# An attention and mixer kernel on one core: another order on SyncE's queue, another scratch for one PSUM copy, one eviction a place earlier, another last piece

## The chip, the cores and the metric

The kernel runs on one core of one Trainium2 chip. The metric is the device time of one execution in microseconds (us), lower is better; a kernel's figure is the median of its runs. Engines are named as the profile names them: PE is TensorE's matmul, PEld its weight loads, DVE is VectorE, ACT is ScalarE, POOL is GpSimd, SP is SyncE. "SPq", "ACTq" and "POOLq" are the queues from which an engine issues DMAs.

## The reference

Two layers in a row, over 8 batches (B), 12 heads (H), 448 tokens (S) and 64 channels a head (D):

```python
def _attn_ref(q, k, v):
    S = q.shape[2]
    scale = 1.0 / np.sqrt(q.shape[-1])
    scores = scale * np.matmul(q, k.transpose(0, 1, 3, 2))
    attn = np.maximum(scores, 0.0) ** 2 / S
    return np.matmul(attn, v)

def _moe_ref(x, w_tok1, w_tok2, w_ch1, w_ch2):      # x: 8 x 448 x 768
    xt = x.transpose(0, 2, 1)
    h = np.maximum(xt @ w_tok1, 0.0) @ w_tok2       # 448 -> 256 -> 448, along the tokens
    u = x + h.transpose(0, 2, 1)
    h2 = np.maximum(u @ w_ch1, 0.0) @ w_ch2         # 768 -> 1536 -> 768, along the channels
    return u + h2
```

The attention has no softmax: a score is cut at zero and squared. Its heads side by side are the 768 channels of x. Inputs and output are float32; the kernel computes in bfloat16 with float32 sums in PSUM.

## The kernel before

**The work.** The heads are taken in 24 groups of four (s = 0 to 23), three groups to a batch. The batches b = 0 to 7 go in pairs p = 0 to 3; a pair has 7 tiles of 128 token rows in the channel layer, 28 over the kernel. The order of all work is written out by hand: `ORDER`, a string of 2024 words, is read from left to right, and each word issues one step on the engine that it names (`:A` on ACT, `:D` on DVE, digits are PSUM banks of a matmul). Each engine runs its steps in that order, with semaphore waits for what each step needs.

**The words.** For a group s:

- `ldk`, `ldq`, `ldv` load k, q and v from POOL (line 371); a name behind a load's colon is a gate: the load is issued once that DMA has landed.
- `ik`, `iq` put k and q in the right layout (ACT or DVE, line 351), `xk`, `xq` transpose them by a DMA on SP (line 497). Groups 0 to 9 are transposed on PE instead.
- `S` are the scores (PE, line 515), `r` their eviction with the cut at zero (line 343 or 345), `q` the squares (355 or 357), `V` the product with v (542), `xe` its eviction (552 or 554).
- `xd` transposes x by a DMA on SP (line 566, tile `x_sb`), from group 6 on; `t1` (PE, line 588) needs it. `rt`, `t2` (597) and `u` (DVE, line 601, tile `uT`) finish the token layer.
- `ub` copies u back into token rows by a DMA transpose on SP (line 610, tile `u_sb`, in the last pair a part of `arena`).

The channel layer's first product is plain for batches 0 and 1 (`C1`, line 623) and a Strassen-like scheme with seven products for the rest (`fast1`): `tu` are sums of u (DVE, line 688), `M1` the products (PE, line 780), `s1` copies of a product from PSUM into a scratch as float32 (ACT, line 793), `d1` the additions that use such a copy and the next product (DVE, line 796). The sums `tu3.0` are made in place in `uT`, so they wait for the `ub` copies of the same u. The second product (`fast2`) takes the tiles of a pair two by two: `h` are sums (688), `M2` products (847), `d2` evictions into the output tile (860 and 862). One tile in seven has no partner (`channel2`): `C2` (PE, line 713) and `c2e` (DVE, line 722). `st` are the stores (line 668), two for a tile of 128 rows, both on SP; in the last pair some are split by columns, and then one half goes from ACT's queue. The tile that ends the list, number 25, is computed in three pieces of columns: `C2.3.4.0` (384 wide), `.1` (256) and `.2` (128).

**SP's queue.** SP issues 152 DMAs in the order of the words: 94 transposes (`xk`, `xq`, `xd`, `ub`) and 58 copies, nearly all of them stores. It is one queue: a DMA whose data isn't there yet holds up those behind it, and each also waits until the DMA eight places ahead of it has landed, since eight semaphores go round.

**Scratch.** The tile `sums` holds, in its last columns, a scratch for a copy of `fast1` (`snaps[0]`, 2 x 448 float32) which shares its place with one of the `tu` sums. In the last pair the array `r2`, the scratches and the sums lie in `arena`, where k, q and their like were. There `fp32(4)` is a view of rows 4 and 5 of `r2`, and the built program's waits go by the stretch of memory that a view spans.

Of the kernel before, what the change touches and what calls it, by code (L numbers as in the profile page):

```python
# [115 lines left out]
V7.2 V7.3 V7.4 r8.6.1:A st1.64 V7.5 c1e1.2:D r8.6.0:A V7.6 S8.4:21 T9.0:56 xe7.1:A r8.4.1:A xe7.0:A S8.1:37  # L116
cp9.0:D C1.1.5:4 r8.1.1:A xd7 r8.1.0:D cp9.1:A C1.1.10:1 r8.4.0:A c1e1.5:D ub1.3 st1.0 q8.2:D S8.5:50 r8.5.1:A
w1.1.1:D S9.0:37 S9.4:64 r8.5.0:A ldv9.0:xd6 ub1.1 xk11 C1.1.9:2 c1e1.9:A r9.4.0:D ldv10.1:st2.64 C1.1.6:0
q8.6:D r9.0.1:A r9.0.0:D w1.1.0:D c1e1.10:D r9.4.1:A C1.1.3:5 xq11 q9.0:D q8.4:D t1.6.0:6 q9.4:A q8.5:A
t1.7.0:3 ldq13.0:st1.0 rt6.0:A iq12:D ub1.2 c1e1.6:A ldk12.1:st1.64 ldq13.1:xd7 c1e1.3:D S9.2:27 rt7.0:A  # L120
S9.3:41 q8.1:D q8.3:D V8.0:56 r9.2.0:D r9.3.0:A V8.1 V8.2 r9.2.1:D S9.1:03 r9.3.1:A V8.3 S9.5:24 r9.1.0:A
r9.1.1:D V8.4 ldk14.0:xk11 S10.1:71 V8.5 r9.5.1:A V8.6 S9.6:03 r9.5.0:D xe8.0:D ldk12.0 ldk15.1 r9.6.0:A
q9.2:A t2.7.0:4 q9.5:D ldk13.0:st1.0 r9.6.1:A C1.1.11:2 q9.1:D ldq15.1 q9.3:A C1.1.7:5 t2.6.0:0 ldk13.1:xq11
q9.6:A xe8.1:D w1.1.2:D r10.1.0:D t2.6.1:3 c1e1.11:A u7.0:D C1.1.8:6 r10.1.1:A u6.0:D q10.1:A c1e1.7:D ub2.0
S10.0:74 V9.0:20 V9.1 V9.2 V9.3 r10.0.0:D c1e1.8:A S10.3:15 u6.1:D V9.4 S10.4:76 xq12 r10.3.1:A ik12:D V9.5
V9.6 h0.3.0:D r10.4.1:A M2.0.3.2:3 xe9.0:D r10.4.0:A st0.0 ub2.1 r10.3.0:A xe9.1:A r10.0.1:D S10.5:56
d2.0.3.11a:D S11.0:72 S11.3:14 q10.3:D r10.5.1:A h0.3.1:D M2.0.3.1:0 r10.5.0:A r11.3.1:D xd8 r11.3.0:A
# [24 lines left out]
q13.4:A M2.1.4.2:5 q13.6:A u10.0:D rt12.0:D xk16 V13.0:32 V13.1 ldq18.0:st3.0 ldk19.0 h1.4.0:D S14.4:17
# [93 lines left out]
def kernel(ctx: ExitStack, tc: tile.TileContext, q: bass.AP, k: bass.AP, v: bass.AP, moe_w_tok1: bass.AP, moe_w_tok2: bass.AP, moe_w_ch1: bass.AP, moe_w_ch2: bass.AP, out: bass.AP):  # L246
    nc = tc.nc
    B, H, S, D = q.shape
# [681 lines left out]
    reads1, reads2 = ({}, {})  # L930
# [73 lines left out]
```

## Time and profile before

| | |
|---|---|
| median of 3 runs | 344.83 us (343.36 to 346.12) |
| the profiled execution, its time | 344.91 us |
| its span, from the first to the last instruction | 342.9 us |
| mean granted TensorE clock | 0.999 |
| PE busy | 333.5 us, 97% of the span |
| DVE, ACT, POOL busy | 295.0, 250.2, 92.0 us (86%, 73%, 27%) |
| PE idle that the waits name | 4.5 us |
| DMA queue of SP and ACT (q1) | 26.92 MB, 44.8% of 16 engines' span |
| DMA queue of POOL (q0) | 21.47 MB, 45.8% |
| out_dram<-out_sb from SP | 42 stores of 192 KB, 3.5 us to landing |
| transposes from SP, u_sb, arena, x_sb | 4.7, 4.7, 5.3 us to landing |

PE is the engine to look at: it is idle for under 10 us of the span. A row of the timeline has the start, the duration, the engine, the line, what is written and read, and in brackets how long the engine had been idle and what ended that. The ends of matmuls are modelled, so a matmul's row ends later than the next one can start; the distance between two starts says more. "DMA share" over 1 means that more packets were under way than there are engines.

### The profile page before, as it was taken

The numbers are of one execution on the slowest core, as the hardware profiler recorded it, in microseconds if no ns is written. First come the engines' busy times: TensorE is split into PE (matmuls) and PEld (weight loads), VectorE is DVE, ScalarE is ACT, GpSimd is POOL, SyncE is SP. The second block draws the span as 40 slices with busy tenths as digits, with TensorE's granted clock in tenths as the row PEclk, the third lists the DMA queues.
The fourth block names the chain that finished last, engine by engine and source line by source line (L and its number), as shares of the span: only waits on it lengthen the run. The fifth ranks groups of instructions, "written<-read, shape, count | busy, mean of one in ns | idle before, by whom it ended". The sixth has DMA issues, their size and how long they took to land.

```text
span 342.9 us, 9412 instructions
## 1 busy us (share of the span) xinstructions
PE 333.5 (97%) x3797; PEld 222.1 (65%) x3797; DVE 295.0 (86%) x571; ACT 250.2 (73%) x462; POOL 92.0 (27%) x157
## 2 busy tenths in 40 slices
PE   8899999999999999999999999999999999999995
PEld 3456655655565658855578556876578777887763
DVE  3999998899899999989898999889986986838783
ACT  4999999858899799879799898979785832221000
POOL 8976422725160343122340712010020000000000
PEclk9999999999999999999999999999999999999999
DMA  8999999999998999999999997897686113432255
GB/s 143 187 176 190 205 210 193 136 153 146 207 184 150 198 132 160 160 208 151 189 171 196 160 179 134 159 151 128 125 135 102 25 31 79 90 80 62 70 149 153
DMA packets 98940, 50.20 MB, mean 146 GB/s; under 512 B 71568, under 2 KB 95952, under 8 KB 98896
## 3 DMA queue, kind: packets, MB, share of 16 engines
q0 software_dynamic: 25136, 21.47, 45.8%
q1 hardware_dynamic: 72736, 26.92, 44.8%
q10 hardware_dynamic: 1024, 1.21, 1.2%
q8 instruction: 29, 0.48, 0.6%
q14 instruction: 15, 0.12, 0.1%
HBM read 43.38 MB, written 11.01 MB: 159 GB/s over the span
## 4 chain that ended last, share of the span: by engine, by line
PE 85%; DMA 5%; POOL 4%; DVE 3%; issue 1%; ACT 1%; SPq 0%; DVEq 0%; ACTq 0%; POOLq 0%
PE m_ps L847 22%; PE m_ps L780 20%; PE sc_ps L515 10%; PE acc_ps L542 8%; PE m_ps L623 8%; PE t_ps L588 6%; PE h_ps L597 5%; PE m_ps L713 4%; POOL arena L371 3%; DMA u_sb<-uT 2%; DMA x_sb<-xT 2%; PE kqT_ps L472 1%; DMA arena<-in_q_dram 1%; PE x_ps L579 1%; DVE arena L796 1%
## 5 line engine op out<-in xcount | busy, mean ns | idle before, releaser
L343 ACT ACTIVATE arena<-sc_ps 128x448 bf16<-128x448 f32 x232 | 117.1, 592 | 17.4 <-PE sc_ps L515 16.8
L355 ACT ACTIVATE arena<-arena 128x896 bf16<-128x896 bf16 x76 | 72.3, 968 | 0.6 <-DVE arena L345 0.3
L345 DVE TENSOR_SCALAR arena<-sc_ps 128x448 bf16<-128x448 f32 x104 | 62.1, 616 | 3.7 <-PE sc_ps L515 3.1
L515 PE MATMUL sc_ps<-arena 64*64 64x448 bf16 x672 | 54.8, 357 | 1.9 <-ACT arena L349 0.8
L357 DVE TENSOR_TENSOR arena<-arena 128x896 bf16<-128x896 bf16 x92 | 55.1, 616 | 1.1 <-ACT arena L343 0.5
L371 POOL DMA_DIRECT2D arena<-in_q_dram x46 | 28.2, 615 | 75.3 <-DMA arena<-arena 28.8
L371 POOL DMA_DIRECT2D arena<-in_v_dram x48 | 29.3, 618 | 66.2 <-DMA arena<-arena 17.5
L780 PEld LDWEIGHTS <-wc 128*128 128x128 bf16 x432 | 40.9, 98 | 5.1 <-issue 2.3
L542 PE MATMUL acc_ps<-arena 64*64 64x448 bf16 x672 | 42.7, 350 | 0.2
L515 PEld LDWEIGHTS <-arena 64*64 64x64 bf16 x672 | 21.7, 105 | 23.9 <-issue 15.4
L371 POOL DMA_DIRECT2D arena<-in_k_dram x48 | 29.7, 623 | 19.4 <-DMA out_dram<-out_sb 9.7
L780 PEld LDWEIGHTS <-ws 128*128 128x128 bf16 x324 | 30.8, 98 | 4.0 <-issue 1.8
L847 PE MATMUL m_ps<-wc,r 128*128 128x384 bf16 x162 | 30.3, 327 | 0.0
L601 DVE TENSOR_TENSOR uT<-h_ps,xT 128x448 bf16<-128x448 f32 x48 | 29.1, 616 | 1.2 <-PE h_ps L597 0.9
L847 PEld LDWEIGHTS <-r 128*128 128x128 bf16 x216 | 20.4, 98 | 14.8 <-issue 2.6
L623 PE MATMUL m_ps<-uT,wc 128*128 128x448 bf16 x144 | 29.9, 353 | 0.0
L542 PEld LDWEIGHTS <-arena 64*64 64x64 bf16 x672 | 20.9, 106 | 11.3 <-issue 3.1
L793 ACT ACTIVATE arena<-m_ps 128x448 f32<-128x448 f32 x18 | 9.3, 542 | 23.7 <-PE m_ps L780 8.3
L588 PE MATMUL t_ps<-x_sb,wt 128*128 128x256 bf16 (+1 forms) x216 | 25.0, 261 | 0.9 <-DMA x_sb<-xT 0.9
L780 PE MATMUL m_ps<-uT,wc 128*128 128x224 bf16 x216 | 25.4, 259 | 0.0
L597 PE MATMUL h_ps<-wt,r_sb 128*128 128x448 bf16 x96 | 25.1, 353 | 0.0
L847 PEld LDWEIGHTS <-sums 128*128 128x128 bf16 x180 | 17.1, 98 | 12.1 <-issue 1.0
(86 smaller groups left out, 510.1 us busy)
## 6 DMA issues: line engine op xcount, KB each, us to landing
out_dram<-out_sb SPq DMA_DIRECT2D x42, 192.0 KB, 3.5
arena<-in_k_dram POOLq DMA_DIRECT2D x48, 112.0 KB, 5.1
arena<-in_v_dram POOLq DMA_DIRECT2D x48, 112.0 KB, 5.2
arena<-in_q_dram POOLq DMA_DIRECT2D x46, 112.0 KB, 4.8
wc<-in_moe_w_ch_dram POOLq DMA_DIRECT2D x6, 768.0 KB, 11.5
out_dram<-arena SPq DMA_DIRECT2D x4, 192.0 KB, 2.7
out_dram<-out_sb SPq DMA_DIRECT2D x8, 96.0 KB, 2.1
out_dram<-out_sb ACTq DMA_DIRECT2D x8, 96.0 KB, 2.4
```

The lines of the kernel that those rows point to most:

```text
L343: nc.scalar.activation(out, ps, AF.Relu)
L345: nc.vector.tensor_scalar(out=out, in0=ps, scalar1=0.0, scalar2=None, op0=ALU.max)
L355: nc.scalar.activation(x, x, AF.Square)
L357: nc.vector.tensor_tensor(out=x, in0=x, in1=x, op=ALU.mult)
L371: o.ins = nc.gpsimd.dma_start(out=raws[t][s % NR][64 * half:64 * (half + 1)], in_=src[b, h0:h0 + 2].rearrange('e (p c) d -> p e (c d)', c=KC))
L515: nc.tensor.matmul(o.ps[e][64 * half:64 * (half + 1), :S], lhsT=lhsT, rhs=rhs, start=True, stop=True, skip_group_check=True)
L542: nc.tensor.matmul(o.ps[half][64 * e:64 * (e + 1), :S], lhsT=r[rows, e, c * D:(c + 1) * D], rhs=sq[rows, e, :], start=c == 0, stop=c == KC ...
L588: nc.tensor.matmul(o.ps[:, j, :], lhsT=wt1[:, c, j * 128:(j + 1) * 128], rhs=x_sb[:, p0:p1, c, :], start=c == 0, stop=c == 3)
L597: nc.tensor.matmul(o.ps[:, :S], lhsT=r1[:, j, a * 128:(a + 1) * 128], rhs=wt2[:, j, :], start=j == 0, stop=j == JC - 1)
L623: nc.tensor.matmul(ps[:, :S], lhsT=wc1[:, g, e * 128:(e + 1) * 128], rhs=uT[:, g, off:off + S], start=g == 0, stop=g == CC - 1)
L780: nc.tensor.matmul(o.ps[:, j * HB:(j + 1) * HB], lhsT=lhs[:, g, (e + j) * 128:(e + j + 1) * 128], rhs=rhs[:, g], start=j == g == 0 and not ...
L847: nc.tensor.matmul(o.ps[:, :HN], lhsT=lhs[:, e], rhs=rhs[:, e], start=e == 0 and not on, stop=e == EC // 2 - 1, skip_group_check=True)
```

## The change

Three words of the table move on the compute engines, about a hundred on SP, and one line of `fast1` changes.

```diff
-V7.2 V7.3 V7.4 r8.6.1:A st1.64 V7.5 c1e1.2:D r8.6.0:A V7.6 S8.4:21 T9.0:56 xe7.1:A r8.4.1:A xe7.0:A S8.1:37
+V7.2 V7.3 V7.4 r8.6.1:A V7.5 c1e1.2:D r8.6.0:A V7.6 S8.4:21 T9.0:56 xe7.1:A ub1.2 r8.4.1:A xe7.0:A S8.1:37
...
                 x, deps = (snaps[k], [got[i, '6'] for i in (0, 2, 4)] if b < 6 else snap_free[k])
             else:
-                x, deps = (fp32(4 if e == 0 else 10), free2)
+                x, deps = (snaps[0], reads1[5] + snap_free[0]) if b == 7 and e == 0 else (fp32(4 if e == 0 else 10), free2)
             a5 = snap('5', x, m5, deps)
```

**SP's queue.** From about the 15th of its DMAs (`st1.64` in the first line above) up to `xd21`, SP's DMAs stand in another order. The loads on POOL keep theirs, but of the 57 that have a gate 38 name another DMA. Here is SP's queue around the transposes of groups 12 to 16, first before: `xq14` and `xq15`, three stores, a `ub`, then `xd12` (`x_sb_70`), a store, `xk15`, a store, `ub3.3` and `ub3.5`, `xk16` and `xq16`, and in the last row `ub3.2` and `ub3.0`.

```order
L497 DMA_TRANSPOSE arena<-arena 128x7x128 x2
L668 DMA out_dram<-out_sb_80 64x768
L668 DMA out_dram<-out_sb_81 64x768
L668 DMA out_dram<-out_sb_79 64x768
L610 DMA_TRANSPOSE u_sb<-uT 128x3x128
L566 DMA_TRANSPOSE x_sb_70<-xT 128x8x128
L668 DMA out_dram<-out_sb_79 64x768
L497 DMA_TRANSPOSE arena<-arena 128x7x128
L668 DMA out_dram<-out_sb_81 64x768
L610 DMA_TRANSPOSE u_sb<-uT 128x4x128 x2
L497 DMA_TRANSPOSE arena<-arena 128x7x128 x2
L610 DMA_TRANSPOSE u_sb<-uT 128x4x128 x2
```

And now, from the stores `st6.64`, `st5.0`, `st5.64`, `st6.0`; then `ub3.0`, `xd11` (`x_sb_71`), `xq14` and `xq15`, `ub3.1`, `xd12` (`x_sb_70`), `xk15`, `ub3.3`, `xq16` and `xk16`, and `ub3.4`, `ub3.2`, `ub3.5`:

```order
L668 DMA out_dram<-out_sb_80 64x768
L668 DMA out_dram<-out_sb_79 64x768 x2
L668 DMA out_dram<-out_sb_80 64x768
L610 DMA_TRANSPOSE u_sb<-uT 128x4x128
L566 DMA_TRANSPOSE x_sb_71<-xT 128x8x128
L497 DMA_TRANSPOSE arena<-arena 128x7x128 x2
L610 DMA_TRANSPOSE u_sb<-uT 128x4x128
L566 DMA_TRANSPOSE x_sb_70<-xT 128x8x128
L497 DMA_TRANSPOSE arena<-arena 128x7x128
L610 DMA_TRANSPOSE u_sb<-uT 128x4x128
L497 DMA_TRANSPOSE arena<-arena 128x7x128 x2
L610 DMA_TRANSPOSE u_sb<-uT 128x4x128 x3
```

The stores that stood among the transposes now stand ahead of them, `ub3.0` has gone from behind `xd12` to ahead of `xd11`, and directly ahead of `xd12` stands `ub3.1` alone.

**The eviction.** `c2e1.6.0` (DVE, line 722), which empties the PSUM bank of the product `C2.1.6.0`, goes one place ahead, past `tu3.0` (line 688, in place in `uT`). The piece of DVE's order, with - for before and + for now:

```order
 L357 TENSOR_TENSOR arena<-arena 128x896
 L601 TENSOR_TENSOR uT<-h_ps,xT 128x448
+L722 TENSOR_TENSOR out_sb_79<-m_ps,u_sb 128x384
 L688 TENSOR_TENSOR uT<-uT 128x3x224
-L722 TENSOR_TENSOR out_sb_79<-m_ps,u_sb 128x384
 L345 TENSOR_SCALAR arena<-sc_ps 128x448 x2
 L688 TENSOR_TENSOR sums<-uT 128x672
```

The eviction and the sum have changed places; the score evictions behind them (line 345) stay where they are.

**The scratch.** For batch 7 the first copy of a fifth product (`s1.7.0.5`) goes into `snaps[0]` in `sums` instead of rows 4 and 5 of the last `r2`; `d1.7.0.22` reads it there. ACT's order around it, with the semaphores that each step waits for, before (the row with x2 holds `s1.6.4.2` and `s1.7.0.5`):

```order
L793 ACTIVATE arena<-m_ps 128x2x224 [waits PE_49]
L793 ACTIVATE arena<-m_ps 128x448
L793 ACTIVATE arena<-m_ps 128x2x224 [waits DVE_49,PE_49] x2
L793 ACTIVATE arena<-m_ps 128x2x224 [waits PE_49]
L793 ACTIVATE arena<-m_ps 128x2x224 [waits DVE_49,PE_49]
```

and now, where `s1.7.0.5` is the row that writes `sums`:

```order
L793 ACTIVATE arena<-m_ps 128x2x224 [waits PE_49]
L793 ACTIVATE arena<-m_ps 128x448
L793 ACTIVATE arena<-m_ps 128x2x224 [waits DVE_49,PE_49]
L793 ACTIVATE sums<-m_ps 128x448 [waits PE_49]
L793 ACTIVATE arena<-m_ps 128x2x224 [waits PE_49]
L793 ACTIVATE arena<-m_ps 128x2x224 [waits DVE_49,PE_49]
```

The order of the steps is the same; the one copy has lost its wait for DVE.

**The last piece.** `C2.3.4.2` (12 matmuls of 128 columns) with its eviction `c2e3.4.2` and its two stores goes from between `M2.3.0.5` and `M2.3.2.1` to the very end, behind `M2.3.2.3`, `d2.3.2.12b` and the stores `st23.1`, which ended the kernel before.

More of the change, by code (lines that the diff above doesn't have):

```diff
@@ new lines @@
+q12.5:A q12.2:D d1.2.0.22:D t1.10.0:5 M1.2.2.3 rt10.0:A q12.1:D d1.2.2.12:D M1.2.0.4 q13.0:A M1.2.2.7 y1.2.0:D
+S13.3:20 d1.2.2.22:D S13.1:75 r13.1.1:D V12.0:41 V12.1 V12.2 r13.3.1:A r13.3.0:A V12.3 V12.4 r13.1.0:A V12.5
+V12.6 q13.3:D S13.5:05 S13.4:27 xe12.1:A r13.5.0:D M1.2.2.4 s1.2.4.1:A xe12.0:D r13.5.1:A M1.2.4.2:1 r13.4.1:D
+ik15:A xd12 M1.2.4.6 M1.2.4.5:0 r13.4.0:D d1.2.4.11:D xk15 y1.2.2:D t2.10.1:4 ldq17.1:ub2.4 ldk17.0 s1.2.4.5:A
+q13.5:D t1.11.0:5 s1.2.4.2:A M1.2.4.3 u10.1:D M1.2.4.7 ub3.3 S13.2:72 d1.2.4.12:D d1.2.4.22:D S13.6:16
```

241 lines of the change are left out of this document (118 added, 123 removed).

## The prediction

> **What bounds the kernel now.** I read the page first, then who PE waited for, then the chain of waits and the timeline where PE waited.
>
> ```profile
> span 342.9 us, 9412 instructions
> PE 333.5 (97%) x3797; PEld 222.1 (65%) x3797; DVE 295.0 (86%) x571; ACT 250.2 (73%) x462; POOL 92.0 (27%) x157
> ...
> PE t_ps L588 <- DMA x_sb<-xT: 0.9, 1, 0.9
> PE sc_ps L515 <- DVE out_sb L722: 0.8, 1, 0.8
> PE m_ps L780 <- ACT arena L793: 0.4, 1, 0.4
> ```
>
> PE is busy for 333.5 of 342.9 us, so at most 9.4 us can be had without taking work from it. This change takes none: it can only fill PE's idle time and shorten what lies behind PE's last matmul. Behind the first group of loads, PE waits three times in the whole span, for 0.9, 0.8 and 0.4 us. The profiled execution took 344.91 us, 2.01 more than its span, and lies 0.08 from the median, 344.83. I work from 344.91 and keep the 2.01.
>
> **SP's queue: the first wait.** Here is PE ahead of that wait, SP's queue over the same time, the eviction on DVE that the transpose needs, and the DMA's own stretch from the chain of waits.
>
> ```profile
> 148.23 0.92 PE L597 MATMUL h_ps<-wt,r_sb 128*128 128x448 bf16 x4
> 150.00 1.05 PE L588 MATMUL t_ps<-x_sb,wt 128*128 128x256 bf16 x8 [0.86 <-DMA x_sb<-xT]
> ...
> 135.53 1.19 SPq L610 DMA_TRANSPOSE u_sb<-uT  x1
> 140.21 1.92 SPq L668 DMA_DIRECT2D out_dram<-out_sb  x3
> 142.17 1.50 SPq L610 DMA_TRANSPOSE u_sb<-uT  x1
> ...
> 142.22 0.61 DVE L554 TENSOR_SCALAR xT<-acc_ps 128x448 bf16<-128x448 f32 x1
> ...
> 143.78 6.18 DMA x_sb<-xT
> DMA to landing us min/median/max: 3.0/5.3/7.5
> 101.71 0.76 PE h_ps L597 x4
> ```
>
> Four matmuls of line 597 take PE 0.76 us, so `t1.12.0` could have started at 148.23 + 0.76 = 148.99; it started at 150.00, and the loss is 1.01 us, of which the row shows 0.86. `xd12` had its data at 142.83, was issued at 143.78 behind three stores and a `ub`, and took 6.18 us. Now only `ub3.1` stands directly ahead of it, the copy that was issued at 135.53 and is through SP long before 142.83. So `xd12` goes out at about 142.9, 0.9 earlier, with the stores gone from ahead of it, and by the shortest, median and longest landing of this kind (3.0, 5.3, 7.5) lands at 145.9, 148.2 or 150.4. PE needs it at 148.99. I take the median, since fewer transfers stand ahead than in the case that took 6.18: the wait goes, 1.01 us by starts, 0.86 by the row. The bounds are a gain of 1.01 and a loss of 0.4.
>
> **The eviction and `ub3.0`: the second wait.**
>
> ```profile
> 163.27 1.46 PE L713 MATMUL m_ps<-wc,r 128*128 128x384 bf16 x8
> 165.45 0.55 PE L542 MATMUL acc_ps<-arena 64*64 64x448 bf16 x8
> 166.78 0.38 PE L515 MATMUL sc_ps<-arena 64*64 64x448 bf16 x4 [0.79 <-DVE out_sb L722]
> 165.75 0.51 DVE L688 TENSOR_TENSOR uT<-uT 128x672 bf16<-128x672 bf16 x1 [1.31 <-DMA u_sb<-uT]
> 166.18 0.55 DVE L722 TENSOR_TENSOR out_sb<-m_ps,u_sb 128x384 f32<-128x384 f32 x1
> 158.02 7.64 DMA u_sb<-uT
> 85.86 1.32 PE acc_ps L542 x28
> ```
>
> DVE sat idle for 1.31 us at `tu3.0`, which waits for the `ub` of 158.02 until 165.66; behind it stood `c2e1.6.0`, though its product had ended at 163.27 + 1.46 = 164.73; and `S15.3` waited for that bank. A matmul of line 542 costs 1.32/28 = 0.047 us, so `S15.3` could have started at 165.45 + 8 x 0.047 = 165.83. It started at 166.78: 0.95 us lost. Both edits hit this. With the eviction first it runs at 164.77 to 165.32, half a microsecond ahead of the need, even if `tu3.0` is as late as before. And `ub3.0`, now ahead of `xd11`, lands well before. Gain 0.79 by the row to 0.95; if either edit failed, the other would still carry it.
>
> **The scratch: the third wait.**
>
> ```profile
> 297.77 0.55 ACT L793 ACTIVATE arena<-m_ps 128x448 f32<-128x448 f32 x1 [4.81 <-DVE arena L796]
> 298.34 0.62 DVE L796 CUSTOM_DVE_ANT_0 arena<-arena,m_ps 128x448 bf16<-128x448 f32 x1 [0.25 <-ACT arena L793]
> 299.06 0.98 ACT L793 ACTIVATE arena<-m_ps 128x448 f32<-128x448 f32 x2 [0.75 <-DVE arena L796]
> 297.94 1.31 PE L780 MATMUL m_ps<-uT,wc 128*128 128x224 bf16 x12
> 299.65 0.73 PE L780 MATMUL m_ps<-uT,ws 128*128 128x224 bf16 x6 [0.40 <-ACT arena L793]
> 219.59 2.87 PE m_ps L780 x30
> ```
>
> `s1.7.0.5` (ACT, 299.06) waited for `d1.6.4.12` (DVE, to 298.96), which writes other columns of the same two rows; the new place in `sums` has no such neighbour, and the built order shows its DVE wait gone. Its product was complete by 298.10, and ACT is free from 297.77 + 0.55 = 298.32, so the copy runs at about 298.35 to 298.90. A matmul of line 780 costs 2.87/30 = 0.096 us, so `M1.7.0.3`, which needs the copy, has its place at 297.94 + 12 x 0.096 = 299.09. Lost before: 0.56 by starts, 0.40 by the row. The cover is thin, 0.19 us, and what comes next is `s1.6.4.2` itself, which waits for DVE as before. Bounds 0 to 0.56.
>
> **The last piece.** PE's work stays the same; its last product is now 12 matmuls of 128 columns.
>
> ```profile
> 324.86 0.50 PE L713 MATMUL m_ps<-wc,arena 128*128 128x128 bf16 x6
> 325.19 0.50 PE L713 MATMUL m_ps<-wc,sums 128*128 128x128 bf16 x6
> 327.17 0.28 DVE L722 TENSOR_TENSOR arena<-m_ps,arena 128x128 f32<-128x128 f32 x1
> 325.52 0.65 PE L847 MATMUL m_ps<-wc,arena 128*128 128x384 bf16 x3
> 337.56 1.14 PE L847 MATMUL m_ps<-wc,arena 128*128 128x384 bf16 x6
> 338.74 0.55 DVE L862 TENSOR_TENSOR out_sb<-out_sb,m_ps 128x384 f32<-128x384 f32 x1 [0.55 <-PE m_ps L847]
> 339.32 0.50 ACTq L668 DMA_DIRECT2D out_dram<-out_sb  x1
> out_dram<-out_sb ACTq DMA_DIRECT2D x8, 96.0 KB, 2.4
> out_dram<-arena ACTq DMA_DIRECT2D x1, 32.0 KB, 2.1
> ```
>
> The piece takes 325.52 - 324.86 = 0.66 us from what stands behind it, so `M2.3.2.3` starts at 336.90 and, its six matmuls lasting 338.70 - 337.56 = 1.14 with 0.97 to the next start, the piece starts at 337.87 and ends at 337.87 + 0.83 (324.86 to 325.69) = 338.70, where PE ended before. Then 0.28 us of eviction instead of 0.55: the store could go at 339.05. But `st23.1` goes out at 338.66 and holds ACT's queue for 0.50, so the last store goes at 339.18 instead of 339.32, 0.14 earlier, and it is 32 KB instead of 96 KB: 2.1 us to landing instead of 2.4. That is 0.4 us; bounds 0.1 (it lands behind the 96 KB all the same) to 0.6. [...]
>
> **What else is moved.** POOL's loads keep their order, but many have another gate; a load that is late holds up all loads behind it. The gates that I followed are DMAs that go out as early as the old ones or earlier (`ldv14.0` waits for `xk15` instead of `ub2.3`), so I cost this at nothing; the cover is PE's other work, and the price if one fails is that of a late transpose below. Stores go out in fours instead of singly. Nothing of this changes PE's order.
>
> **The sum.** By the rows 0.86 + 0.79 + 0.40 = 2.05 us, by starts 1.01 + 0.95 + 0.56 = 2.52; the middle is 2.3, and 0.4 from the end. 344.91 - 2.7 = 342.2 us. Ends with all bounds: 344.91 - 2.52 - 0.6 = 341.8 and, with the first term lost, the third at 0 and 0.1 at the end, 344.91 + 0.4 - 0.79 - 0.1 = 344.4.
>
> **The rivals.**
>
> ```profile
> 131.00:150.00 19.00, 18.15 (x204) 14.94 (x196) 18.01 (x36) 16.57 (x32) 4.47 (x8) 1.00 1.29 181
> 222.00:234.00 12.00, 12.00 (x145) 9.33 (x144) 10.22 (x20) 9.34 (x20) 1.78 (x3) 1.00 1.25 163
> ...
> 224.33 0.98 ACT L552 ACTIVATE xT<-acc_ps 128x448 bf16<-128x448 f32 x2
> 233.60 1.04 PE L588 MATMUL t_ps<-x_sb,wt 128*128 128x256 bf16 x8
> ```
>
> These two are windows: length, then busy PE, PEld, DVE, ACT, POOL, the clock, the DMA share, GB/s.
>
> *DVE takes the wait over.* In 131 to 150 DVE is busy 18.01 of 19 us: it can't run more than 1 us ahead, so PE, with its first wait gone, would meet DVE instead. For: that share. Against: DVE itself loses 1.31 us of idle time at 165.75 and waits less for stores. Price: the first term goes and half of the second with it, 1.0 + 0.4 = 1.4 less gain: 343.6 us. Chance 0.20.
>
> *The queue's moves change nothing on PE,* and the transposes still come late because the DMA engines are full (share 1.29): then the eviction, the scratch and the end alone pay, 0.79 + 0.40 + 0.4: 343.3 at best, 344.4 with the bounds above; I take 344.0. Chance 0.10.
>
> *Stores in fours hold up the transposes behind them: slower.* Ahead of `xd19` now stand four stores of 192 KB, 0.79 MB, 4.8 us at the 163 GB/s of its window. Its data is there at 224.33 + 0.98 = 225.31, `t1.19.0` uses it at 233.60: 8.3 us. At the median landing, 5.3 + 4.8 = 10.1, PE would wait 1.8 us, at the longest, 12.3, 4.0. `xd15` stands likewise behind two stores. With two such waits of 1.8 to 4.0 us the gain of 2.7 turns: it decides when they add to more than 2.7. I price it at 4.5: 344.91 - 2.7 + 4.5 = 346.7. Against: `xd12` had three stores and a `ub` directly ahead and took 6.18, not 10. Chance 0.08. [...]
>
> *More than the sum.* Loads and evictions that come earlier also shorten PE's waits below what the view shows as idle; the distance between rows and starts above, 2.52 - 2.05, shows that such time exists. Another 1.2 us: 341.0. Chance 0.08.
>
> **How the numbers follow.** The forecast has the other 0.54, at 342.2, its own range 341.4 to 343.0. The runs of before lie 2.8 us apart, so each case is smeared by about 0.7 us. A change of 1%, about what a measurement of this kernel can tell, is 3.4 us: faster below 341.4, slower above 348.3. Faster: most of the last case and a sixth of the forecast, 0.06 + 0.09 = 0.15. Slower: the far end of the third rival, 0.03, and 0.01 for what I did not see. Within: 0.81. The range from 341.1 to 344.6 leaves out the slower rival, half of the last case and a tenth of the rest.
>
> **What would show it.** In the changed kernel's waits of PE, the three rows (x_sb, out_sb L722, arena L793) are gone or below 0.2; `t1.12.0` starts within 0.1 us of the end of its forerunners; DVE's 1.31 at `tu3.0` is gone; ACT's copy into `sums` starts right behind the copy ahead of it; the last row is a 32 KB store. PE's busy time stays at 333 us while the span falls to 340.2. Wrong would be: a new wait of PE for x_sb near 186 or 233, which means the third rival; DVE above 98% from 131 to 150 with PE waiting for line 345 or 796, the first; the same x_sb row, the second.

## The result, and the profile after

The changed kernel takes 354.70 us in the median of six runs (351.77 to 359.67), the kernel before 344.29 (343.20 to 346.12): a ratio of 1.0247, with a 95% interval from 1.020 to 1.0294. The ratio, here and below, leaves out slow executions, those over 1.5% above the fastest of their kernel, so it is not the quotient of the two medians. The forecast was 342.2 with a range from 341.1 to 344.6, so it was wrong in sign: not 2 us faster but 10.4 us slower by the medians, 8.5 by the ratio. The profiled execution, the shortest of the six, took 351.77 us at a span of 349.9, 7.0 more than before. Here are the head of its page, with the granted clock in 40 slices, and the first rows of who PE waited for.

```profile
span 349.9 us, 9436 instructions
PE 336.7 (96%) x3797; PEld 223.1 (64%) x3797; DVE 295.1 (84%) x571; ACT 250.4 (72%) x462; POOL 91.9 (26%) x157
...
PEclk9999999999998799999999999999999999999999
```

```profile
PE sc_ps L515 <- DVE xT L554: 4.4, 1, 4.4
PE t_ps L588 <- DMA x_sb<-xT: 1.2, 2, 0.8
```

Two of the three old waits are gone (`out_sb L722` and `arena L793`), the one for `x_sb` is still there at 0.8, and one stands that the kernel before did not have: 4.4 us for line 554 on DVE (`xe9.0`, which empties the PSUM bank that the scores `S11.0` write next). Behind it the clock falls, in two slices, to 0.8 and 0.7. Since PE runs the same steps in the same order until close to the end, the start of one step in both traces says how far the changed kernel lags:

| step on PE | before | after | lag |
|---|---|---|---|
| `t1.7.0` | 95.33 | 96.48 | 1.15 |
| `S11.3` | 107.03 | 112.80 | 5.8 |
| `S11.1` | 109.78 | 118.54 | 8.8 |
| `t1.12.0` (first old wait) | 150.00 | 158.99 | 9.0 |
| `S15.3` (second) | 166.78 | 174.81 | 8.0 |
| `M1.7.0.3` (third) | 299.65 | 306.80 | 7.15 |
| end of the span | 342.9 | 349.9 | 7.0 |

So the loss arises almost whole between 105 and 119 us. About 4.6 us of it is PE's idle time, and 3.0 more come in the 6 us right behind, without any wait. DVE's timeline shows what PE waited for: `u6.1` and the cast `ik12`, behind which come a sum and `xe9.0`. First before, then after:

```profile
104.50 0.61 DVE L601 TENSOR_TENSOR uT<-h_ps,xT 128x448 bf16<-128x448 f32 x1
105.03 0.38 DVE L351 COPY arena<-arena 128x896 bf16<-128x896 bf16 x1
```

```profile
105.66 0.61 DVE L601 TENSOR_TENSOR uT<-h_ps,xT 128x448 bf16<-128x448 f32 x1
111.34 0.39 DVE L351 COPY arena<-arena 128x896 bf16<-128x896 bf16 x1 [5.07 <-issue]
```

The cast `ik12` (line 351) stood for 5.07 us. ("issue" means that the view names nothing that ended the wait.) It needs the load `ldk12.0`, and the trace has that load landed at 111.27 us, 0.07 before. In the kernel before it landed at 103.75, 1.28 us ahead of `ik12`. It is one of nine loads that POOL issues in a row. Here are the k-loads among them, by the DMAs issued from 95.5 to 101.6 before, and from 98.4 to 104 after (the last number is the median time to landing):

```profile
arena<-in_k_dram POOLq DMA_DIRECT2D x6, 112.0 KB, 4.8
```

```profile
arena<-in_k_dram POOLq DMA_DIRECT2D x6, 112.0 KB, 10.4
out_dram<-out_sb SPq DMA_DIRECT2D x3, 192.0 KB, 5.7
...
arena<-arena SPq DMA_TRANSPOSE x1, 10.5
x_sb<-xT SPq DMA_TRANSPOSE x1, 13.7
```

And SP's queue over that time, before and after:

```profile
96.61 7.81 SPq L610 DMA_TRANSPOSE u_sb<-uT  x2
104.52 2.08 SPq L497 DMA_TRANSPOSE arena<-arena  x1
```

```profile
97.75 2.52 SPq L668 DMA_DIRECT2D out_dram<-out_sb  x4
100.44 1.42 SPq L497 DMA_TRANSPOSE arena<-arena  x1
102.26 3.19 SPq L566 DMA_TRANSPOSE x_sb<-xT  x1
105.55 6.99 SPq L610 DMA_TRANSPOSE u_sb<-uT  x3
```

Before, `ub2.0` stood ahead of `xq12` and held the queue until its data came: the first `ub` of the row of 7.81 us was issued at 96.61, the second at 103.24, and between them SP sent nothing. POOL's nine loads ran in that gap. After, four stores, `xq12` and `xd8` go out in it. The nine start 2.7 us later besides (98.55 instead of 95.86), since the first of them, `ldq13.0`, has another gate (`xq11`, landed at 98.00, instead of `st1.0`, at 95.31). Two windows, 104 to 108 before and after, and those behind (the two numbers ahead of GB/s are the clock and the DMA share):

```profile
104.00:108.00 4.00, 4.00 (x59) 2.10 (x52) 4.00 (x9) 3.86 (x10) 0.00 (x0) 1.00 0.76 136
```

```profile
104.00:108.00 4.00, 4.00 (x55) 1.97 (x54) 1.98 (x4) 3.82 (x9) 0.00 (x0) 1.00 1.53 126
108.00:110.00 2.00, 0.35 (x5) 0.00 (x0) 0.00 (x0) 1.23 (x3) 0.00 (x0) 1.00 1.68 153
110.00:112.00 2.00, 0.00 (x0) 0.00 (x0) 0.66 (x2) 0.00 (x0) 0.00 (x0) 0.93 1.19 86
112.00:118.00 6.00, 5.21 (x23) 2.10 (x26) 4.92 (x11) 2.42 (x4) 0.59 (x1) 0.50 1.39 170
118.00:119.00 1.00, 1.00 (x13) 0.29 (x6) 0.46 (x1) 0.38 (x2) 0.00 (x0) 0.72 0.48 46
```

From 104 to 108 fewer bytes moved (126 GB/s against 136) at twice the DMA share (1.53 against 0.76). PE then stands from 108.35 to 112.79, and from 112 to 118 the granted clock is 0.50: that is the second part of the loss. Six matmuls of one shape take 1.15 us ahead of the wait and 2.10 behind it:

```profile
106.71 1.15 PE L847 MATMUL m_ps<-wc,r 128*128 128x384 bf16 x6
...
112.79 1.12 PE L515 MATMUL sc_ps<-arena 64*64 64x448 bf16 x7 [4.44 <-DVE xT L554]
113.84 2.10 PE L847 MATMUL m_ps<-wc,r 128*128 128x384 bf16 x6
```

### The profile page after: what moved, and what is told of

It is laid out like the page before. It is cut to its first block, busy times and chain, and to the rows that moved or that the text cites. A ratio compares the mean times of both kernels' runs of the same rounds, so it can differ in the third digit from the quotient of the medians.

```text
span 349.9 us, 9436 instructions
## 1 busy us (share of the span) xinstructions
PE 336.7 (96%) x3797; PEld 223.1 (64%) x3797; DVE 295.1 (84%) x571; ACT 250.4 (72%) x462; POOL 91.9 (26%) x157
## 3 DMA queue, kind: packets, MB, share of 16 engines
q10 hardware_dynamic: 1024, 1.21, 1.2%
## 4 chain that ended last, share of the span: by engine, by line
PE 86%; DMA 5%; ACT 4%; issue 2%; DVE 1%; POOL 0%; DVEq 0%; POOLq 0%
PE m_ps L847 24%; PE m_ps L780 21%; PE sc_ps L515 10%; PE acc_ps L542 8%; PE m_ps L623 6%; PE t_ps L588 5%; PE h_ps L597 5%; PE m_ps L713 4%; ACT arena L343 3%; DMA x_sb<-xT 2%; DMA arena<-arena 2%; DMA arena<-in_k_dram 2%; PE kqT_ps L472 1%; PE warm_ps L414 1%; PE x_ps L579 1%
## 5 line engine op out<-in xcount | busy, mean ns | idle before, releaser
L515 PE MATMUL sc_ps<-arena 64*64 64x448 bf16 x672 | 55.6, 362 | 6.0 <-DVE xT L554 4.4
L371 POOL DMA_DIRECT2D arena<-in_k_dram x48 | 29.9, 632 | 16.3 <-DMA arena<-arena 10.4
L847 PE MATMUL m_ps<-wc,r 128*128 128x384 bf16 x162 | 31.3, 334 | 0.0
L793 ACT ACTIVATE arena<-m_ps 128x448 f32<-128x448 f32 x17 | 8.8, 542 | 23.2 <-PE m_ps L780 8.5
```

The lines of the kernel that those rows point to most:

```text
L371: o.ins = nc.gpsimd.dma_start(out=raws[t][s % NR][64 * half:64 * (half + 1)], in_=src[b, h0:h0 + 2].rearrange('e (p c) d -> p e (c d)', c=KC))
L515: nc.tensor.matmul(o.ps[e][64 * half:64 * (half + 1), :S], lhsT=lhsT, rhs=rhs, start=True, stop=True, skip_group_check=True)
L847: nc.tensor.matmul(o.ps[:, :HN], lhsT=lhs[:, e], rhs=rhs[:, e], start=e == 0 and not on, stop=e == EC // 2 - 1, skip_group_check=True)
```

## The experiments

**Which part of the change it is.** First the changed kernel with the old queue and the old gates; the edit, seen from the kernel before, is this:

```diff
+c2e1.6.0:D
 tu3.0:D
...
-c2e1.6.0:D
...
-C2.3.4.2:0
...
-c2e3.4.2:D
...
-st25.2.64
...
-st25.2.0
...
 st23.1.0
+C2.3.4.2:0 c2e3.4.2:D st25.2.64 st25.2.0
...
-x, deps = (fp32(4 if e == 0 else 10), free2)
+x, deps = (snaps[0], reads1[5] + snap_free[0]) if b == 7 and e == 0 else (fp32(4 if e == 0 else 10), free2)
```

> The changed kernel with SyncE's old queue and POOL's old gates: the eviction ahead of tu3.0, the snapshot's new scratch and the last piece at the end stay. Theory Q (the queue alone makes the kernel slower; the load ldk12.0 that DVE's cast ik12 needs is issued late and lands 10.4 us later instead of 5.2): no PE wait near 108, granted clock 1.00 throughout, waits for out_sb L722 and arena L793 gone (-0.9 and -0.5), the 0.9 us wait for x_sb still there, about 0.2 at the end: 344.3 - 1.6 = 342.7 us. Rival R (the scratch in sums or the moved eviction holds DVE up, and the queue is innocent): about 354, with DVE idle 5 us at ik12.

Measured: 344.52 us (343.20 to 346.86) against 345.47 for the kernel before on that chip, a ratio of 0.9983 (0.9948 to 1.0018). The span of the profiled execution is 341.5. Its first row of PE's waits:

```profile
PE sc_ps L515 <- DVE out_sb L860: 1.3, 1, 1.3
```

No hole (no standstill of PE) near 108, clock 1.000, and neither `L722` nor `L793` among PE's waits: the queue's new order is not needed for these two. The 1.3 us are new. DVE's `d2.1.4.11a` waits for the store `st3.0`, which here goes out at 147.94 although its data was there at 120.10. In this execution `xd12` landed at 147.74, before its need, and what was late next was that store. The same kernel again:

> The same kernel as in the first call (old queue; eviction, scratch and last piece as changed), timed again because 0.998 with an interval from 0.995 to 1.002 does not tell a gain of 1.6 us from none. If the gain read off the trace there (1.0 and 0.9 us at the two waits, 0.2 at the end, less up to 1.3 where DVE waits for st3.0) is real: 0.994 to 0.998 again. If run-to-run waits for DMAs eat it: 0.998 to 1.001.

Measured: 346.83 us (343.66 to 349.77) against 345.70, ratio 1.0009 (0.9968 to 1.0049), span 342.4, and both waits gone again. A gain of 1 us can be read off the traces, but the two timings don't show one. The other half alone, SP's new order and POOL's new gates with the eviction, the scratch and the last piece as before; the edit is the one above with its signs turned, in the changed kernel:

> The kernel before with SyncE's new queue and POOL's new gates, and nothing else of the change. Theory Q: the whole loss, PE idle 4 to 5 us near 108 for DVE's L554 behind ik12, a granted clock of 0.5 for some 6 us after it; 354.7 plus what the other three parts give (0.4 to 0.8): 355 to 356 us. Rival R: 344 us.

Measured: 356.64 us (355.25 to 360.05), ratio 1.031 (1.024 to 1.0379). PE's waits in the profiled execution, the longest of the four:

```profile
PE t_ps L588 <- DMA x_sb<-xT: 3.8, 2, 3.5
PE sc_ps L515 <- DVE xT L554: 3.7, 1, 3.7
PE sc_ps L515 <- DMA arena<-arena: 3.2, 1, 3.2
```

The queue with its gates makes the whole loss, and the wait for `out_sb` (line 722) is gone here too, without the eviction's move. And the hole near 108 is not alone: `S14.0` waits 3.2 us for `xq14`, `t1.16.0` 3.5 for `xd16`.

**What makes the loads late at the first hole: the gate, the stores or the transposes.** The gate:

```diff
-ldq13.0:xq11
+ldq13.0:ub1.1
```

> The changed kernel with one gate changed: POOL's load ldq13.0, the first of the nine loads issued from 98.55, waits for ub1.1 (landed at 95.4) instead of xq11 (98.0), so all nine go out about 2.6 us earlier. Theory G (the late gate makes the loss): ldk12.0 goes out at 98.2, ahead of most of the four stores, and takes 5 to 6 us: 104, before DVE wants it at 106.3; no PE wait there, clock 1.00: 354.7 - 7.5 = 347.2 us. Theory S (the four stores and the transposes behind them fill the DMA engines whenever the loads go out): ldk12.0 takes 8 to 10 us, lands at 106 to 108, DVE waits up to 2 us, and ik13 behind it for ldk13.1 as well; 348.5 to 351 us.

Measured: 349.64 us (348.11 to 352.00), ratio 1.0126 (1.0065 to 1.0188). Three loads went out from 94.52, but the next, `ldk14.0`, has `xk11` for its gate, which landed only at 101.50 beside them: `ldk12.0` was issued at 102.61, later than in the changed kernel, took 6.2 us, and PE stood 2.1 us instead of 4.4, with the clock at 1.00. So what `ldk12.0` gained, it did not gain by going out earlier. That the spread of the loads helped it is argued, not shown. The four stores:

```diff
-ub1.3 st1.64 st1.0 st0.64 st0.0 xq12 xd8 ub2.2 ub2.0 ub2.1
+ub1.3 xq12 xd8 ub2.2 ub2.0 ub2.1 st1.64 st1.0 st0.64 st0.0
-ldk13.1:st1.0
+ldk13.1:xk11
```

> The changed kernel with the four stores st1 and st0 put behind ub2.1 on SyncE's queue, and ldk13.1's gate, a store, replaced by xk11; POOL's loads still start behind xq11. Theory S (the stores fill the engines): ldk12.0 goes out at 100.9, takes 5 to 6 us, lands at 106 to 107: a wait of DVE of under 1 us instead of 5.1, no loss of clock, 354.7 - 7 = 347.7 us. Theory G (the gate): the same loads go out no earlier, so the wait stays at 2 us or more: 350 us or more. Third, the transposes and not the stores slow the loads: with xq12 and xd8 sent even sooner ldk12.0 still takes 10 us, and the time stays at 354.

Measured: 352.11 us (349.27 to 355.29), ratio 1.0164 (1.0095 to 1.0234). In the profiled execution, the longest of the four, `ldk12.0` took 7.0 us instead of 10.4, later ones 10.2; PE stood 1.6 us there, 1.8 a little later, and 2.9 for `xd12`. Neither the gate nor the stores alone are the cause. Now the gap itself is put back, and nothing else:

```diff
-st1.0 st0.64 st0.0 xq12 xd8 ub2.2 ub2.0 ub2.1
+st1.0 ub2.0 st0.64 st0.0 xq12 xd8 ub2.2 ub2.1
```

> The changed kernel with ub2.0 moved ahead of st0.64, st0.0, xq12, xd8 and ub2.2 on SyncE's queue: it waits for u6.0 until about 104.3, and behind it, as in the kernel before, nothing goes out from 99 to 104.3, while POOL's nine loads run. The gates stay. Theory F (the old queue's wait at ub2.0 kept SyncE still during the nine loads, and filling that gap with stores and transposes is what slows the loads): ldk12.0, issued at 100.9, takes 5 to 6.5 us and lands at 106 to 107.4, DVE's wait falls from 5.1 to at most 1.1 us, the clock stays at 1.00; later waits for x_sb and xq14 stay: 354.7 - 6.5 = 348 us. Rival G (the late gate): 2 us or more of DVE's wait stay, 350 us or more. Rival T (later waits make most of the loss): above 351 us.

Measured: 351.61 us (347.55 to 353.44), ratio 1.0175 (1.0113 to 1.0237). The k-loads issued from 98 to 103.6, and PE's first wait:

```profile
arena<-in_k_dram POOLq DMA_DIRECT2D x6, 112.0 KB, 5.9
```

```profile
PE t_ps L588 <- DMA x_sb<-xT: 5.7, 2, 4.4
```

The first hole is gone, though the late gate stayed: with SP still from 98.8 to 104.0, the loads take 5.9 us. The gain did not reach the end. PE, now earlier, met `xd12`: SP needed from 144.30 to 150.61 to issue it, it landed at 154.81, PE stood for 4.4 us and the clock fell to 0.50 again. Then the reverse, in the kernel before: the gap filled with the transposes alone,

```diff
-ub1.2 ub2.0 xq12 st0.0 ub2.1 xd8 st0.64
+ub1.2 xq12 xd8 ub2.0 st0.0 ub2.1 st0.64
...
-ldv11.0:xq12 ldv11.1:xq12 ldv10.0:xq12
+ldv11.0:st0.0 ldv11.1:st0.0 ldv10.0:st0.0
```

> The kernel before with xq12 and xd8 alone moved ahead of ub2.0, so that they go out at 99 and 101 instead of 104.5 and 108.6, into the gap (and the three gates on xq12 put on st0.0, which lands when xq12 did). Theory F, transposes: the loads issued from 95.9 to 100.8 take 7 to 10 us where they took 4.7 to 5.9, ldk12.0 lands at 105.5 to 108, DVE waits for it or for ldk13.1 by 1 to 4 us, and PE by up to 3 us: 345 to 350 us against 344.6. Rival G (the gate alone): the gate is the old one, so no wait near 107 and 344.6 us or less.

and with the two stores alone:

```diff
-ub1.2 ub2.0 xq12 st0.0 ub2.1 xd8 st0.64
+ub1.2 st0.0 st0.64 ub2.0 xq12 ub2.1 xd8
```

> The kernel before with the two stores st0.0 and st0.64 alone moved ahead of ub2.0, so that they go out at 98 and 98.6 instead of 106.7 and 110.0, into the gap. If stores are what slows the loads: ldk12.0 takes 7 us or more, DVE waits 1 us or more. If the transposes are: ldk12.0 takes 5 to 6 us, no wait of over 0.5 us near 105, and with less in the queue behind it xd8 lands a microsecond earlier: 344.0 to 345 us.

Measured, the transposes: 345.46 us (343.95 to 348.66), ratio 1.0052 (1.0019 to 1.0085), so half a per cent slower; PE idle 1.4 us behind `ik12`, and 1.8 us at `t1.7.0`, ahead of the place that was changed. The stores: 344.51 us (343.05 to 350.72), ratio 1.0005 (0.997 to 1.0041), no such wait. The k-loads of the same row of nine, transposes first, then stores:

```profile
arena<-in_k_dram POOLq DMA_DIRECT2D x6, 112.0 KB, 8.3
```

```profile
arena<-in_k_dram POOLq DMA_DIRECT2D x6, 112.0 KB, 6.2
```

With SP still the k-loads took 4.8 us in the kernel before and 5.9 in the run with the gap put back; two stores make 6.2, two transposes 8.3, and all of it 10.4. Each is one execution. The transposes stand clear of the 4.8 to 5.9, the two stores hardly do; that stores add to transposes is seen where the four were taken away, 7.0 instead of 10.4 for `ldk12.0`. By their shapes the two transposes move 0.49 MB (128x7x128 and 128x8x128 in bf16) and the two stores 0.39, so the transposes weigh more than their bytes, in these two executions. That SP's stillness in this gap protected the loads is shown from both sides: with it put back the loads took 5.9 us instead of 10.4; with the gap of the kernel before filled by the two transposes they took 8.3 instead of 4.8.

**What a hole costs.** Twelve, and then six, multiplications of a small tile by itself were put on DVE ahead of `ik12` in the kernel before:

```diff
-ik12:D
+pause0:D pause1:D ... pause11:D ik12:D
```

> The kernel before, with twelve multiplications of a 128x608 tile by itself put on DVE ahead of ik12, the instruction that waited in the changed kernel; no DMA is moved. They take 4.5 to 5 us. If a standstill of DVE here costs PE its length less what is buffered (0.7 us in the changed kernel: 5.1 on DVE, 4.4 on PE) and then half the clock for 6 us, as the changed kernel's windows show: PE idle 3.8 to 4.3 us near 107, clock 0.5 for some 6 us, 344.7 + 7 = 351 to 352 us. If the low clock came from the full DMA engines and not from PE's idle time: no low clock, 348.5 us.

> The same with six of them, 2.3 to 2.5 us: PE idle 1.4 to 2 us near 107, less than the 2.08 us that left the clock at 1.00 in the run with the early gate: 344.7 + 1.7 = 346.4 us. If the clock falls after short waits as well: 348 us or more.

Measured: twelve took 6.07 us; PE stood from 107.74 to 113.00; 351.50 us (350.72 to 352.58), ratio 1.0167 (1.0109 to 1.0226). Six took 3.01 us; PE stood 2.21; 347.86 us (346.17 to 349.11), ratio 1.0063 (1.0027 to 1.010). The windows of the run with six:

```profile
110.00:112.00 2.00, 1.62 (x13) 0.82 (x13) 2.00 (x5) 0.82 (x2) 0.60 (x1) 1.00 0.91 175
112.00:114.00 2.00, 2.00 (x8) 0.76 (x5) 2.00 (x5) 1.83 (x3) 1.39 (x3) 0.50 1.05 190
114.00:115.00 1.00, 1.00 (x13) 0.37 (x12) 0.73 (x2) 0.00 (x0) 1.00 (x3) 0.50 1.27 217
115.00:116.00 1.00, 1.00 (x12) 0.36 (x5) 0.00 (x0) 0.45 (x2) 0.59 (x1) 0.80 1.18 163
```

No DMA was moved here, and behind PE's idle time the clock stood at 0.50 all the same, from 112 to 115. Against the trace of before, PE's lag grows behind the hole by 2.5 us with twelve (6.16 at `S11.0`, 8.63 at `S10.6`) and by 1.4 with six (3.39, 4.80). I had expected the six to leave the clock alone; that was wrong.

**Whether the loss sits in a few places.** With the first place mended as above, the second was mended too, and then the second without the first:

```diff
-ub2.4 ub2.3 st3.64
+ub2.4 st3.64
...
-ub2.5 st6.64 st5.0 st5.64 st6.0 ub3.0 xd11 xq14 xq15 ub3.1 xd12 xk15 ub3.3
+ub2.5 st5.0 st5.64 xd11 xq14 xq15 ub3.1 xd12 xk15 ub2.3 ub3.0 st6.64 st6.0 ub3.3
```

> The changed kernel with SyncE's queue mended at two places: ub2.0 again ahead of st0.64, st0.0, xq12, xd8 and ub2.2 (the first place), and ub2.3, ub3.0, st6.64 and st6.0 moved from ahead of xd11 and xd12 to behind xk15 (the second). Gates and everything else as in the changed kernel. Theory F (the new queue loses where it sends work of no hurry ahead of or beside DMAs that are due, at these two places): no wait of PE over 1 us after the first 20 us, clock 1.00, xd12 landed within 0.5 us of its need: 343.5 us, a ratio to the kernel before of 0.990 to 1.002. Rival T (the new queue loses at more places, each time another): still 1.005 or more.

> The changed kernel with the second place alone mended: ub2.3, ub3.0, st6.64 and st6.0 behind xk15. Theory F: the hole at ik12 stays (PE idle 4 to 4.5 us near 109, then half the clock), about 7.5 us: 351 to 353 us, a ratio of 1.02. If the first place is only one of many, or PE's delay there only hides the second, the ratio is above 1.03 or below 1.01.

Measured: both, 355.08 us (351.35 to 357.11), ratio 1.0246 (1.0184 to 1.0309); the second alone, 357.25 (356.07 to 361.20), ratio 1.0369 (1.029 to 1.0449), with the hole near 108 still there (3.8 us) and one of 4.4 for a load of v. The first row of PE's waits in the run with both:

```profile
PE acc_ps L542 <- DMA arena<-in_v_dram: 6.3, 2, 6.1
```

A third load, `ldv15.1`, was late by 6.1 us. It is gated on the store `st11.64` and was issued at 176.76 where PE needed it about 178. In the kernel before it was gated on `xd13`, issued at 169.89, and landed 1.21 us before its use. So it was given back `xd13`, by way of `ldk19.1` just ahead of it on POOL, and two transposes of no hurry went behind `xk17`; in a further run the next late load, `ldk18.1`, was freed too, by taking away the gate of `ldv16.0` ahead of it on POOL, which is the last pair of lines here:

```diff
-ldq19.1:xk17 ldk19.1:st11.64 ldv15.1:st11.64
+ldq19.1:xq16 ldk19.1:xd13 ldv15.1
...
-xk16 ub3.4 ub3.2 ub3.5 xd13 xk17
+xk16 ub3.2 xd13 xk17 ub3.4 ub3.5
...
-ldv16.0:xq17
+ldv16.0
```

> The kernel with two places mended, and the third mended as well: ldv15.1, the load that V15.1 waited 6.1 us for there, is released by xd13 as in the kernel before (ldq19.1 by xq16) and not by the store st11.64, and the transposes ub3.4 and ub3.5, needed 30 us later, go behind xk17. Theory L (a handful of due loads and transposes, each to be found by its wait): no wait of PE over 1.5 us left, clock 1.00, 345 us, ratio 0.996 to 1.004. Theory T (the new queue is full of such places, and each that is mended brings PE to the next one earlier): another wait of 2 us or more at a new place, ratio 1.01 or more.

> The kernel with three places mended and one more gate taken away: ldv16.0, which stood in front of ldk18.1 on POOL's queue, no longer waits for xq17 (landed at 176.40), so that ldk18.1, for which DVE's ik18 waited from 177.9 to 184.8, goes out behind ldk20.1 near 170 instead of 178.1. Theory L (the loss sits in the few loads and one transpose that had the least to spare in the kernel before: ldk12.0 1.28 us, ldv15.1 1.21, ldk18.1 0.08, and xd12, late already): no wait of PE over 1.5 us, clock 1.00 throughout, 349.0 - 5.8 (its idle 5.4 us at S16.2 and the rest of the clock, as the lag at t2.13.0 shows, less what the waits at V15 and xd12 vary) = 343.5 to 345.5 us, ratio 0.995 to 1.003. Theory T (every stretch of the new queue has such a place): a fifth one of 2 us or more, ratio 1.008 or more.

Measured: three places, 352.52 us (350.89 to 353.32), ratio 1.0192 (1.015 to 1.0233); four, 352.97 (350.25 to 354.47), ratio 1.0246 (1.019 to 1.0302). The first row of PE's waits with three, and with four:

```profile
PE sc_ps L515 <- DVE xT L554: 5.4, 1, 5.4
```

```profile
PE sc_ps L515 <- DMA arena<-arena: 2.6, 1, 2.6
PE t_ps L588 <- DMA x_sb<-xT: 2.5, 3, 0.9
```

With three places mended PE reached `S17.1`, at 176.54, 0.16 us ahead of the kernel before, and then lost 5.4 us and the clock to `ldk18.1`, issued at 178.12 instead of 172.22. With four, no wait is over 2.65 us, but the loads issued from 168 to 174 take 8 to 10 us, and a transpose, `xq17`, was late. So mending one place at a time, four times, did not bring the time back: each place that was mended let PE arrive earlier at the next. Lastly, all 57 gates away, in the changed kernel; the first two of the nine loads for all:

```diff
-ldq13.0:xq11 ldk12.1:ub1.2
+ldq13.0 ldk12.1
```

> The changed kernel without any gate on POOL's loads of q, k and v: each goes out when POOL reaches it and its buffer is free. Theory G2 (the new gates, which release the loads in a burst behind a late DMA, make the loss): ldk12.0 and ldv15.1 land several us ahead of their need, no hole near 108, 346 to 348 us. Theory F (what matters is how much runs beside the loads and the due transposes, whoever goes first): the loads come earlier, but now run beside other transposes: the holes move, waits for x_sb or xq of 1 to 4 us appear, 348 to 356 us.

Measured: 363.44 us (357.30 to 365.40), against 345.70 for the kernel before; the executions lie too far apart for a ratio. The first row of PE's waits, and the k-loads and two kinds of transposes issued from 89 to 106:

```profile
PE t_ps L585 <- DMA x_sb<-xT: 15.7, 5, 10.2
```

```profile
arena<-in_k_dram POOLq DMA_DIRECT2D x7, 112.0 KB, 9.1
...
arena<-arena SPq DMA_TRANSPOSE x3, 11.4
...
x_sb<-xT SPq DMA_TRANSPOSE x1, 11.8
```

Now `ldk12.0` is early (issued at 91.65, landed at 101.01), and `t1.7.0` waits 10.2 us for `xd7`. In this execution, without gates, the one `x_sb` transpose of that time took 11.8 us, against a median of 5.3 in the kernel before: the gates held the loads off the transposes, as the gap held the transposes off the loads.

**An order by need in one place only.** The old queue with the three other edits, and an order by need only between `xd11` and `ub3.3`:

```diff
-xd11 ub3.1 xq14 xq15 st6.64 st3.64 st5.0 ub2.3 xd12 st5.64 xk15 st3.0 ub3.3
+xd11 xq14 xq15 ub3.1 st3.64 st3.0 ub2.3 xd12 st6.64 st5.0 st5.64 xk15 ub3.0 ub3.3
...
-ldv14.0:ub2.3
+ldv14.0:xd12
...
-ldq18.0:st3.0
+ldq18.0:ub3.3
```

> The old queue with the three other edits (eviction, scratch, last piece) and the new principle in one place only, between xd11 and ub3.3: xq14 and xq15 ahead of ub3.1, st3.64, st3.0 and ub2.3 ahead of xd12, st6.64 and st5.0 behind it, ub3.0 behind xk15; POOL's gates on ub2.3 and st3.0 put on xd12 and ub3.3, which keeps its loads where they were. Theory F (an order by need helps where it lays nothing on loads that are due): xd12 lands by 148.5 at the latest and no PE wait for x_sb stands at t1.12.0, the 1.3 us that S14.3 lost behind the late st3.0 is gone, S15.3 and M1.7.0.3 stay without waits: 344.5 - 1.0 to 1.5 = 343.2 us, a ratio to the kernel before of 0.994. Rival D (DVE at 95% of this stretch takes every wait over): new waits of PE for DVE between 147 and 167 of 0.8 us or more together, ratio 0.998.

Measured: 344.46 us (342.70 to 347.01), ratio 1.0008 (0.9972 to 1.0045), span 341.5. In the trace all goes as expected up to `S15.3`, 2.0 us ahead of the kernel before; then `V15.0` loses 0.9 us to a load of v and `t1.16.0` 0.3 to an `xd`, and the median shows no gain. No version beat the kernel before.

## Why the prediction was wrong, step by step

*What else is moved: the step that failed.* The prediction costed POOL's gates at nothing because "the gates that I followed" go out as early as the old ones, and named one of 38. It asked when a load is released and left out what runs beside it: that the old queue's wait at `ub2.0` kept SP still while nine loads ran was in no term. In the changed kernel, with that gap filled, `ldk12.0` took 10.4 us instead of 5.2, and PE lost 4.4 us of waiting and 3.0 to the clock. With the gap put back and the new gates kept, `ldk12.0` took 5.8 us and the hole was gone. The gate of `ldq13.0`, 2.7 us later by its DMA's landing, was not among those named either; made early, with the gap still filled, it left PE standing for 2.1 us. The trace of before had the warning: of its loads after 60 us, those that landed less than 1.3 us ahead of their use were `ldk9.1` (0.88), `ldk12.0` (1.28), `ldv15.1` (1.21) and `ldk18.1` (0.08). Three of these four became holes of 4 us and more in one run or another. The cover named, "PE's other work", was the 1.28 us that `ldk12.0` had in hand and some 0.6 us between DVE's wait and PE's (5.07 and 4.44).

*The price of a failed cover* was put at that of a late transpose, 1.8 to 4.0. The wait was 4.4, and the clock added 3.0; PE's busy time, forecast to stay at 333 us, went to 336.7. PE's granted clock stood at 0.999 in the whole trace of before, and nothing in the prediction asked what idle time does to it. With the clock counted, a wait of 4.0 us would have been priced near 7 (an estimate: the 4.0 and the 3.0 that the clock added here).

*The first wait.* Wrong. Its row is still there, 0.8 us. The prediction had `xd12` go out as soon as its data was there, since `ub3.1` ahead of it "was issued at 135.53": that was its time in the old queue. In the new one it stands behind `xq14` and `xq15` and was issued from 150.68 to 152.69, `xd12` at 152.79, 1.25 us after its data. The chain of waits gives its landing:

```profile
152.79 6.15 DMA x_sb<-xT
```

The median of 5.3 was assumed, "since fewer transfers stand ahead"; it was as slow as before. Nor was the wait a fixed loss of the old queue: in the two profiled executions of the old queue with the three other edits `xd12` took 3.11 and 4.97 us, and PE did not wait for it. A wait read from one execution was taken for one of every execution.

*The second wait.* Right: between `t1.12.0` and `S15.3` the lag falls from 8.99 to 8.03, 0.96 us, against 0.79 to 0.95. The eviction runs ahead of `tu3.0` (line 688), and `S15.3` follows without a wait. Either edit does it alone, as the prediction said: the first run has the eviction without the queue, the run of the queue alone has the queue without the eviction, and in neither does PE wait for line 722.

```profile
173.75 0.56 DVE L722 TENSOR_TENSOR out_sb<-m_ps,u_sb 128x384 f32<-128x384 f32 x1 [0.34 <-PE m_ps L713]
174.23 0.50 DVE L688 TENSOR_TENSOR uT<-uT 128x672 bf16<-128x672 bf16 x1
```

*The third wait.* Right: 0.57 us by the lag (from 7.72 at the matmul ahead to 7.15 at `M1.7.0.3`), against 0.40 to 0.56, with ACT's copy into `sums` directly behind the copy ahead:

```profile
305.48 0.54 ACT L793 ACTIVATE arena<-m_ps 128x448 f32<-128x448 f32 x1 [4.80 <-DVE arena L796]
305.92 0.54 ACT L793 ACTIVATE sums<-m_ps 128x448 f32<-128x448 f32 x1
```

*The last piece.* Right within its bounds. PE's last matmuls and the last store:

```profile
345.43 0.50 PE L713 MATMUL m_ps<-wc,sums 128*128 128x128 bf16 x6
...
346.47 0.79 ACTq L668 DMA_DIRECT2D out_dram<-arena  x1
```

PE ends at 345.93, 349.9 - 345.93 = 4.0 us ahead of the end, where before it was 342.9 - 338.70 = 4.2. That is 0.2, not 0.4. Of it 0.08 come from the store's going out sooner behind PE's end (0.54 instead of 0.62) and 0.18 from its landing (2.18 us instead of 2.36): in this one pair the smaller store landed sooner, by less than the 0.3 of the rows.

*The rivals.* The slower one, of stores that go out in fours, had the sign, a chance of 0.08, and half the mechanism: what collides is SP's queue with POOL's loads, in both directions (in the changed kernel's first gap the k-loads took 10.4 us, the transposes beside them 10.5 and 13.7), two transposes weigh more than two stores (8.3 us for the loads beside them against 6.2), and the places are `ldk12.0`, `xd12` and `ldv15.1`, not `xd15` and `xd19`. "DVE takes the wait over" was seen once, without the queue's change: 1.3 us at `d2.1.4.11a`, and there DVE itself waited for a store. The sign of the second rival, the same `x_sb` row, is there, but the queue's moves did change PE's time, for the worse.

*What stays open.* The profiled execution lost 7.0 us, the medians differ by 10.4: the others must have had further waits, as those of the queue alone did, but they have no trace. The new order with the old gates was not run, so the shares of the two in the whole loss are not told apart. And why this order as a whole crowds the DMA engines at one time (a share of 1.53 from 104 to 108), where the old one did not (0.76), was shown for the first gap alone; for the later places it was argued from the rows of single loads.

## What to carry to other kernels

A queue that stands still may be what keeps another queue's transfers on time, so an order by need has to count the other queues' transfers that are due in the same microseconds (here six k-loads took 4.8 us beside a still SP and 10.4 beside four stores and two transposes). Before moving DMAs or gates, list for every load how long ahead of its use it landed, and follow those with the least to spare first. Price a wait of the matrix engine with the clock behind it: here 4.4 us of waiting cost 7.4.

## What the runs showed of the hardware

Loads of 112 KB took 4.8 and 5.9 us to landing with SP still, 6.2 beside two stores, 8.3 beside two transposes and 10.4 beside four stores and two transposes. Each is the median of six k-loads in one execution. From 104 to 108 us the changed kernel moved fewer bytes at twice the DMA share of the kernel before (126 GB/s at 1.53 against 136 at 0.76).

The time that the granted clock stood at 0.50 is worked out from the windows: for each, twice its length times what the clock lacks to 1.00 (an estimate that has the clock at 1.00 or 0.50 and nowhere between). By the windows shown with the result this is 6.8 us in the changed kernel. The windows of the run with three places mended give 3.4 (behind the length stands PE's busy time, third from the end the clock):

```profile
184.00:186.00 2.00, 0.21 (x3) 0.13 (x3) 1.19 (x3) 0.00 (x0) 0.00 (x0) 0.86 1.43 172
186.00:188.00 2.00, 2.00 (x15) 0.83 (x12) 1.42 (x3) 1.06 (x3) 0.00 (x0) 0.50 1.21 233
188.00:189.00 1.00, 1.00 (x6) 0.63 (x5) 0.19 (x1) 1.00 (x3) 0.00 (x0) 0.57 1.02 205
189.00:190.00 1.00, 1.00 (x12) 0.92 (x10) 1.00 (x3) 1.00 (x2) 0.00 (x0) 1.00 0.79 153
```

So the length of a wait alone doesn't give its price. Here a wait of 5.4 us was followed by 3.4 us at half the clock, in the changed kernel one of 4.4 by 6.8, with the gap put back one of 4.4 by 6.8 as well, and in the queue alone one of 3.7 by 3.4. A wait of 2.21 us was enough with the six multiplications, with 3.4 us at 0.50; one of 2.08 was not with the early gate, where the clock is 1.00 in every window from 108 to 116.
